# Order edges that hold background work behind a step's own operations, in a kernel of attention and two MoE layers on one core

## Chip, core and metric

One core of a Trainium2 chip runs the whole program in one launch. The metric is the device time in microseconds (us) of an execution; a kernel's time is the median of its runs.

## What is computed

Attention on q, k, v of 2 batches, 8 heads, 576 positions and 64 channels feeds a dense layer with a SiLU gate, and that one feeds four experts:

```python
q_d, k_d, v_d = (a.reshape(B, H, S // 4, 4, D).mean(axis=3) for a in (q, k, v))
out_up = np.repeat(sm_attn(q_d, k_d, v_d), 4, axis=2)
# local part: softmax over the keys with |i - j| < 4
x = (out_up + out_local).transpose(0, 2, 1, 3).reshape(1152, 512)
h = x @ w_in                                     # 512 x 2048
x = (h * (1.0 / (1.0 + np.exp(-h)))) @ w_out     # 2048 x 512
p = domain_probs / (domain_probs.sum(-1, keepdims=True) + 1e-09)
for e in range(4):                               # w1[e] 512 x 1024, w2[e] 1024 x 512
    out += p[:, e:e + 1] * (np.maximum(x @ w1[e], 0.0) @ w2[e])
```

## The kernel before

Every large product runs on TensorE (PE) from fp32 operands that are split in two: a rounded high part and the rest (h and l). A product is three matmuls, high by high, high by low and low by high (`mm3`, L468; `prod`, L667). A split is a copy on ScalarE (ACT) and a subtraction on VectorE (DVE) or POOL. The PSUM tiles of the first-layer products rotate over three banks (`mm_tile`).

The first layer runs in two halves of its 2048 hidden channels (`hf`), each over four chunks of tokens of 256, 320, 256 and 320 (`ci`). For a chunk, eight steps `g1_step` (12 matmuls) make a hidden tile each: ScalarE takes a Tanh (L487), VectorE makes the gate (L488), and one step later (`pend`, `flush`) ScalarE and VectorE split it (L493, L494). Four steps `g2_step` (24 matmuls) then multiply by w_out. In the first half ScalarE stores their result (L520), in the second VectorE adds it (L523), and ScalarE and VectorE split the sum as the experts' input (L524, L525).

An expert `e` takes four chunks of tokens (`ci`, 256 tokens, the last 384), and for each chunk four blocks of hidden channels (`k`). `first_products` makes a block (24 matmuls), ScalarE takes the ReLU (L644), four sums of quarter tiles follow (`SUMS`, L649: all on POOL for k of 0 and 1; for k of 2 and 3 three on VectorE and one on POOL), and ScalarE and VectorE split the result in two parts (L651, L652). `second_products` (21 matmuls, L667) multiplies seven combinations with seven w2 blocks, a block scheme that saves an eighth of the matmuls. `outputs` adds the chunk on VectorE (L693 to L728).

Beside the running step the weights are made ready. Pieces of the first layer's weights are loaded as 64-bit words and decoded (`split_raw`, L165 to L172). Pieces of the first expert's w1 come through the same queue of pieces (units 8 and 9, four pieces): a copy (L175) and a subtraction (L176), called by `split_ok` in the main loop once `limit` allows their unit. w2 blocks are loaded by `stage_ahead` (L558), which also makes the four block sums of a w2 block (L568, on POOL, for block 3 on VectorE) as soon as a block is staged and one of two `ks` tiles is free. `split_kk` splits a w2 block in four parts (L596; L598 on VectorE, the first part of each on POOL). `split_u` does the same for w1 of later experts (L580, L582).

No order is written out by hand: a scheduler places the instructions of each engine by data dependencies, by its own model of times and by a priority, which `prio` and `at_prio` set from a step's number. Each engine then runs its list strictly in that order.

## Time and profile before

| | us |
|---|---|
| median of 3 runs | 707.71 |
| lowest, highest of the runs | 705.44, 708.93 |
| profiled execution, its own time | 708.98 |
| its span from the first to the last instruction | 707.2 |

In the profile L12 is line 12 of the kernel. PE is the matmul, PEld the weight load of TensorE, SP the engine that issues the DMAs. A matmul's end in the profile is modelled, so that two in a row overlap. In the words after an instruction, [1.52 <-DVE gf L488] says that its engine had stood idle for 1.52 us and that an instruction of line 488 on VectorE ended that. Granted clock is the share of TensorE's full clock, 1.00 for the upper of its two levels and 0.50 for the lower.

### The profile page before, as it was taken

To read this page: it belongs to the slowest core of one execution; us is meant where nothing else is said; L and a number is where in the kernel's file an instruction comes from. 1 tells how busy PE (TensorE), PEld (TensorE's weight loads), DVE (VectorE), ACT (ScalarE), POOL (GpSimd) and SP (SyncE) were. 2 spreads that over 40 slices of the span, in tenths; PEclk is the share of its full clock that TensorE was granted. 3 is DMA by queue.
4 is the path that set the end of the run, shared out by engine and by line. 5 is a ranking of instruction groups with operands and counts; after the bars stand their busy time and mean duration, and the time that the engine had idled before them with its cause. 6 is when DMAs were issued, how large, how long until landed. Compare 5 with 4: busy or idle time off the path is not lost.

```text
span 707.2 us, 13791 instructions
## 1 busy us (share of the span) xinstructions
PE 668.5 (95%) x5516; PEld 649.8 (92%) x5516; DVE 445.1 (63%) x882; ACT 332.6 (47%) x753; POOL 248.9 (35%) x346
## 2 busy tenths in 40 slices
PE   5777999999989999998999999999999999999996
PEld 4565899999889999998999999999999999999995
DVE  5988747546864434674555886538866559755444
ACT  4667646457763422543334643335533356433321
POOL 4574442114420000365324482136542244322210
PEclk9978999999999999999999999999999999999999
DMA  9875532005461000032001420003210010000001
GB/s 260 246 220 196 164 94 64 22 12 168 137 201 32 1 1 1 1 123 87 1 1 33 139 69 1 1 1 112 99 31 1 1 53 9 1 32 16 17 31 44
DMA packets 16927, 48.16 MB, mean 68 GB/s; under 512 B 2976, under 2 KB 4256, under 8 KB 16864
## 3 DMA queue, kind: packets, MB, share of 16 engines
q1 hardware_dynamic: 16864, 47.29, 21.4%
q8 instruction: 43, 0.70, 0.4%
q14 instruction: 20, 0.16, 0.1%
HBM read 44.93 MB, written 2.36 MB: 67 GB/s over the span
## 4 chain that ended last, share of the span: by engine, by line
PE 79%; DMA 8%; DVE 6%; ACT 3%; issue 2%; POOL 2%; SPq 0%; DVEq 0%; POOLq 0%; ACTq 0%
PE mm L468 49%; PE p L667 25%; DMA stg<-in_w_dram 5%; DVE dec L169 2%; DMA kst<-in_w2d_dram 2%; DVE dec L167 1%; PE s L303 1%; POOL wbuf L172 1%; DMA vg<-in_va_dram 1%; PE o L395 1%; PE t L363 1%; ACT dec L165 1%; PE o L391 1%; DVE gl L494 1%; ACT stg L166 1%
## 5 line engine op out<-in xcount | busy, mean ns | idle before, releaser
L468 PE MATMUL mm<-xh,wbuf 128*128 128x256 f32 (+2 forms) x1280 | 274.6, 299 | 5.5 <-ACT xh L407 2.8
L468 PEld LDWEIGHTS mm<-xh,wbuf 128*128 128x128 f32 x1280 | 214.2, 192 | 7.2 <-DVE gf L488 3.6
L468 PE MATMUL mm<-xl,wbuf 128*128 128x256 f32 (+2 forms) x640 | 191.0, 299 | 0.0
L649 POOL TENSOR_TENSOR r<-r 128x128 f32<-128x128 f32 x160 | 93.5, 595 | 190.9 <-ACT r L644 150.9
L652 DVE TENSOR_TENSOR h<-r,h 128x384 fp32r<-128x384 f32 (+1 forms) x128 | 89.8, 702 | 72.5 <-ACT h L651 72.2
L468 PEld LDWEIGHTS mm<-xl,wbuf 128*128 128x128 f32 x640 | 122.5, 191 | 0.3
L651 ACT ACTIVATE h<-r 128x384 fp32r<-128x384 f32 (+1 forms) x128 | 73.9, 578 | 87.2 <-POOL r L649 57.2
L468 PE MATMUL mm<-gh,wbuf 128*128 128x256 f32 (+1 forms) x512 | 104.7, 297 | 0.9 <-ACT acc L520 0.9
L667 PE MATMUL p<-wext,h 128*128 128x256 f32 x672 | 96.1, 284 | 2.4 <-ACT h L651 2.4
L667 PEld LDWEIGHTS p<-wext,h 128*128 128x128 f32 x672 | 87.6, 191 | 2.8 <-ACT h L651 2.8
L667 PE MATMUL p<-wbuf,h 128*128 128x256 f32 x672 | 85.4, 280 | 0.0
L468 PEld LDWEIGHTS mm<-gh,wbuf 128*128 128x128 f32 x512 | 82.6, 188 | 1.2 <-ACT acc L520 1.2
L667 PEld LDWEIGHTS p<-wbuf,h 128*128 128x128 f32 x672 | 82.0, 188 | 0.0
L468 PE MATMUL mm<-gl,wbuf 128*128 128x256 f32 (+1 forms) x256 | 74.6, 297 | 0.0
L644 ACT ACTIVATE r<-mm 128x512 f32<-128x512 f32 x48 | 28.6, 597 | 82.4 <-PE mm L468 82.4
L649 DVE TENSOR_TENSOR r<-r 128x128 f32<-128x128 f32 x96 | 33.4, 348 | 40.7 <-ACT r L644 36.3
L494 DVE TENSOR_TENSOR gl<-gf,gh 128x256 fp32r<-128x256 f32 (+1 forms) x64 | 35.9, 562 | 19.6 <-ACT gh L493 19.4
L468 PEld LDWEIGHTS mm<-gl,wbuf 128*128 128x128 f32 x256 | 47.8, 188 | 0.1
L172 POOL TENSOR_TENSOR wbuf<-dec,wbuf 128x512 fp32r<-128x512 f32 x24 | 32.4, 1354 | 33.1 <-ACT wbuf L171 26.0
L598 POOL TENSOR_TENSOR wext<-kst,wext 128x512 fp32r<-128x512 f32 x8 | 10.6, 1325 | 85.0 <-issue 72.9
L695 DVE SCALAR_TENSOR_TENSOR acc<-p,pr,acc 128x256 f32<-128x256 f32 (+1 forms) x63 | 36.3, 604 | 6.5 <-PE p L667 6.5
L493 ACT ACTIVATE gh<-gf 128x256 fp32r<-128x256 f32 (+1 forms) x64 | 28.2, 441 | 19.0 <-DVE gf L488 19.0
(122 smaller groups left out, 989.0 us busy)
## 6 DMA issues: line engine op xcount, KB each, us to landing
stg<-in_w_dram SPq DMA_DIRECT2D x32, 512.0 KB
kst<-in_w2d_dram SPq DMA_DIRECT2D x16, 512.0 KB
kst<-in_w1d_dram SPq DMA_DIRECT2D x12, 512.0 KB
kq<-in_kqa_dram SPq DMA_DIRECT2D x8, 419.0 KB
kq<-in_kqb_dram SPq DMA_DIRECT2D x8, 323.0 KB
vg<-in_va_dram SPq DMA_DIRECT2D x8, 288.0 KB
stg<-in_w1d_dram SPq DMA_DIRECT2D x4, 512.0 KB
vw<-in_vb_dram SPq DMA_DIRECT2D x8, 180.0 KB
```

The source lines that it names most:

```text
L169: DVE.scalar_tensor_tensor(out=ai, in0=v[:, :, 1], scalar=-2 ** 31, in1=ai, op0=ALU.bitwise_and, op1=ALU.bitwise_or)
L172: POOL.tensor_tensor(out=l[:, c], in0=a, in1=h[:, c].bitcast(F32), op=ALU.subtract)
L468: ins = [PE.matmul(out=ps, lhsT=l, rhs=r, start=(first and i == 0), stop=(last and i == n - 1)) for i, (l, r) in enumerate(pairs)]
L493: ACT.activation(out=gh[ft][:, 0:n], in_=gf[:, 0:n], func=ACTF.Copy)
L494: DVE.tensor_tensor(out=gl[ft][:, 0:n], in0=gf[:, 0:n], in1=gh[ft][:, 0:n].bitcast(F32), op=ALU.subtract)
L598: eng.tensor_tensor(out=l[:, r], in0=x, in1=h[:, r].bitcast(F32), op=ALU.subtract)
L644: ACT.activation(out=r[:, 0:4].rearrange("p s t -> p (s t)"), in_=ps[:, 0:512], func=ACTF.Relu)
L649: (DVE if k in FAST_K and o != 7 else POOL).tensor_tensor(out=r[:, o], in0=r[:, a], in1=r[:, b], op=op)
L651: ACT.activation(out=h, in_=r[:, part], func=ACTF.Copy)
L652: DVE.tensor_tensor(out=l, in0=r[:, part], in1=h.bitcast(F32), op=ALU.subtract)
L667: ins = [PE.matmul(out=ps, lhsT=x, rhs=y, start=(opens and k == 0 and i == 0), stop=(k == 3 and i == n - 1), skip_group_check=True) for i, ...
L695: DVE.scalar_tensor_tensor(out=o, in0=ps, scalar=p, in1=o, op0=ALU.mult, op1=ALU.add)
```

## The change

A table `latest` keeps, for each engine, the last operation of the running step: the split of a hidden tile, of the first layer's sum, and the quarter sums and subtractions of an expert's block. `behind` adds an order edge from that operation to one of background work; the edge sets the order on the engine's list and adds no semaphore. Three kinds of background work get it: the pieces of the first expert's w1, the splits of w2 blocks 2 and 3 of the first expert, and all block sums. The pieces of w1 are besides taken up at four set steps, the odd ones of the second chunk in the second half, where `split_ok` had taken them up as they came. The block sums leave `stage_ahead` for a function `sum_ahead`, called at set places: for the first expert at the end of the first layer, for a later one in chunk 2 of the expert before (blocks 0 and 1) and in its chunk 3 after a w2 block was split (blocks 2 and 3).

```diff
--- before.py
+++ after.py
@@ -106,6 +106,18 @@
         return 96 + EXPERT * ((u - 8) // 2) + (0, 4)[u % 2]
 
 
+    latest = {}
+
+    def follow(i, earlier, reason):
+        tc.add_manual_dep(i.ins, earlier.ins.name, mybir.DependencyInfo(mybir.DependencyClass.NoSync, mybir.DependencyReason.DATA),
+                          reason=reason)
+
+    def behind(eng, i):
+        if eng in latest:
+            follow(i, latest[eng], "background work")
+        return i
+
+
 
     pieces = deque([(u, j) for u in range(8) for j in range(4)] + [(u, j) for u in range(8, 10) for j in range(2)])
     loaded = deque()
@@ -172,8 +184,8 @@
             POOL.tensor_tensor(out=l[:, c], in0=a, in1=h[:, c].bitcast(F32), op=ALU.subtract)
         else:
             c = slice(j * 1024, (j + 1) * 1024)
-            ACT.activation(out=h[:, c], in_=t, func=ACTF.Copy)
-            DVE.tensor_tensor(out=l[:, c], in0=t, in1=h[:, c].bitcast(F32), op=ALU.subtract)
+            behind(ACT, ACT.activation(out=h[:, c], in_=t, func=ACTF.Copy))
+            behind(DVE, DVE.tensor_tensor(out=l[:, c], in0=t, in1=h[:, c].bitcast(F32), op=ALU.subtract))
 
 
     actx = ExitStack()
@@ -289,8 +301,7 @@
 
 
     def after(i, earlier):
-        tc.add_manual_dep(i.ins, earlier.ins.name, mybir.DependencyInfo(mybir.DependencyClass.NoSync, mybir.DependencyReason.DATA),
-                          reason="PSUM bank")
+        follow(i, earlier, "PSUM bank")
 
     def local_scores(j):
         nb = j.nb
@@ -490,8 +501,8 @@
         flush()
 
         def fin():
-            ACT.activation(out=gh[ft][:, 0:n], in_=gf[:, 0:n], func=ACTF.Copy)
-            DVE.tensor_tensor(out=gl[ft][:, 0:n], in0=gf[:, 0:n], in1=gh[ft][:, 0:n].bitcast(F32), op=ALU.subtract)
+            latest[ACT] = ACT.activation(out=gh[ft][:, 0:n], in_=gf[:, 0:n], func=ACTF.Copy)
+            latest[DVE] = DVE.tensor_tensor(out=gl[ft][:, 0:n], in0=gf[:, 0:n], in1=gh[ft][:, 0:n].bitcast(F32), op=ALU.subtract)
 
         pend.append(fin)
 
@@ -521,8 +532,8 @@
         else:
             yf = tmp_p.tile([128, 320], F32, tag="gf", name="gf")
             DVE.scalar_tensor_tensor(out=yf[:, 0:n], in0=ps[:, 0:n], scalar=0.5, in1=ya, op0=ALU.mult, op1=ALU.add)
-            ACT.activation(out=xh[:, db, c], in_=yf[:, 0:n], func=ACTF.Copy)
-            DVE.tensor_tensor(out=xl[:, db, c], in0=yf[:, 0:n], in1=xh[:, db, c].bitcast(F32), op=ALU.subtract)
+            latest[ACT] = ACT.activation(out=xh[:, db, c], in_=yf[:, 0:n], func=ACTF.Copy)
+            latest[DVE] = DVE.tensor_tensor(out=xl[:, db, c], in0=yf[:, 0:n], in1=xh[:, db, c].bitcast(F32), op=ALU.subtract)
 
 
 
@@ -557,7 +568,10 @@
             with at_prio(need_of(e, x, k) - LEAD_KLOAD):
                 SP.dma_start(out=t.rearrange("p (s c) -> p s c", c=256) if x == "k" else t,
                              in_=w2d[e, k] if x == "k" else w1d[e, :, 1024 * k:1024 * k + 1024])
-        while sums_todo and sums_todo[0] in staged and ks_p and len(sums) < 2:
+
+    def sum_ahead(e, k):
+        if (e, k) in ((e, k) for e, x, k in sums_todo):
+            assert sums_todo[0] == (e, "k", k) and len(sums) < 2
             key = sums_todo.popleft()
             t = staged[key][0].rearrange("p (s c) -> p s c", c=256)
             c = sums[key] = ks_p[0].tile([128, 3, 256], F32, tag="ks", name="ks")
@@ -565,7 +579,7 @@
             with at_prio(need_of(*key) - LEAD_KSUM):
                 for o, a, b in ((c[:, 2], t[:, 3], t[:, 0]), (t[:, 3], t[:, 2], t[:, 3]),
                                 (c[:, 0], t[:, 2], c[:, 2]), (c[:, 1], t[:, 1], c[:, 0])):
-                    eng.tensor_tensor(out=o, in0=a, in1=b, op=ALU.subtract)
+                    behind(eng, eng.tensor_tensor(out=o, in0=a, in1=b, op=ALU.subtract))
 
     def home_u(k):
         h, l = slot(8 + k // 2)
@@ -593,9 +607,12 @@
         parts = (slice(2, 4), slice(4, 6), slice(0, 2), slice(6, 7))
         for part, (r, x) in enumerate(zip(parts, (t[:, 0:2], t[:, 2:4], c[:, 0:2], c[:, 2:3]))):
             with at_prio(tick_of(e, 0, k) + 6 - LEAD_KSPLIT):
-                ACT.activation(out=h[:, r], in_=x, func=ACTF.Copy)
+                a = ACT.activation(out=h[:, r], in_=x, func=ACTF.Copy)
                 eng = POOL if (k, part) in LO_ON_POOL else DVE
-                eng.tensor_tensor(out=l[:, r], in0=x, in1=h[:, r].bitcast(F32), op=ALU.subtract)
+                b = eng.tensor_tensor(out=l[:, r], in0=x, in1=h[:, r].bitcast(F32), op=ALU.subtract)
+                if e == 0 and k > 1:
+                    behind(ACT, a)
+                    behind(eng, b)
         wk[k] = (h, l)
         held[i] -= 1
         stage_ahead()
@@ -646,10 +663,11 @@
             with at_prio(p + d):
                 if n == 1:
                     for o, a, b, op in SUMS:
-                        (DVE if k in FAST_K and o != 7 else POOL).tensor_tensor(out=r[:, o], in0=r[:, a], in1=r[:, b], op=op)
+                        eng = DVE if k in FAST_K and o != 7 else POOL
+                        latest[eng] = eng.tensor_tensor(out=r[:, o], in0=r[:, a], in1=r[:, b], op=op)
                 h, l = (x[:, part.start - 1:part.stop - 1] for x in st.h)
                 ACT.activation(out=h, in_=r[:, part], func=ACTF.Copy)
-                DVE.tensor_tensor(out=l, in0=r[:, part], in1=h.bitcast(F32), op=ALU.subtract)
+                latest[DVE] = DVE.tensor_tensor(out=l, in0=r[:, part], in1=h.bitcast(F32), op=ALU.subtract)
 
     def bank(i):
         return pp_p[0].tile([128, 512], F32, tag=f"p{i}", name=f"p{i}")
@@ -789,7 +807,11 @@
                     g1_step(u0, ft, ci)
                 if hf == 0 and ci < 3:
                     attn_tick()
-                split_ok(limit[0])
+                if hf == 1 and ci == 1 and ft % 2:
+                    limit[0] = 10
+                    split_ok(10)
+                elif limit[0] < 10:
+                    split_ok(limit[0])
             flush()
             if hf == 0 and ci == 2:
                 close_attn()
@@ -798,19 +820,20 @@
                 u5_p[0].close()
                 ks_p.append(ctx.enter_context(tc.tile_pool(name="ks", bufs=2)))
                 stage_ahead()
-                for k in range(2):
-                    split_kk(0, k)
+                for k in range(4):
+                    sum_ahead(0, k)
+                    if k < 2:
+                        split_kk(0, k)
             if ci == 3:
-                limit[0] = 8 if hf == 0 else 10
+                limit[0] = 8
             for db in range(4):
                 next_step()
                 g2_step(u0 + 2, hf, db, ci)
                 if hf == 0 and ci < 2:
                     attn_tick()
-                split_ok(limit[0])
-                split_ok(limit[0])
-            if hf == 0 and ci == 3:
-                limit[0] = 10
+                if limit[0] < 10:
+                    split_ok(limit[0])
+                    split_ok(limit[0])
     while loaded:
         split_piece()
     m1ctx.close()
@@ -838,6 +861,8 @@
         second_products(st, ch)
         if ci == 3 and e < NE - 1:
             split_kk(e + 1, k)
+            if k < 2:
+                sum_ahead(e + 1, k + 2)
         if k == 3:
             outputs(e, ci, ch, p)
 
@@ -851,6 +876,8 @@
                 first_products(st)
                 if ci == 3 and e < NE - 1:
                     split_u(e + 1, k)
+                if ci == 2 and k % 2 == 0 and e < NE - 1:
+                    sum_ahead(e + 1, k // 2)
                 if before:
                     finish(*before, tick_of(e, ci, k) + (3 if ci == 3 else 2))
                 before = (st, ch)
```

Below, the lists of the engines as the build puts them, with line numbers of the file they are from (the changed file has L175 as L187, L487 as L498, L493 as L504, L520 as L531, L524 as L535, L568 as L582, L596 as L610, L644 as L661, L649 as L667, L651 as L669). Numbers behind a name tell apart tiles of one kind.

ScalarE before, from the last stores of the first half (acc) to the first steps of the second (th is a Tanh, gh a copy, stg a piece of w1, kst a block of w2):

```order
L520 ACTIVATE acc_75<-mm_2546 128x320
L175 ACTIVATE wbuf_76<-stg_2588 128x1024
L175 ACTIVATE wbuf_76<-stg_2623 128x1024
L175 ACTIVATE wbuf_76<-stg_2632 128x1024
L520 ACTIVATE acc_75<-mm_2590 128x320
L487 ACTIVATE th_2647<-mm_2634 128x256
L175 ACTIVATE wbuf_76<-stg_2653 128x1024
L493 ACTIVATE gh0_77<-gf_2648 128x256
L487 ACTIVATE th_2668<-mm_2655 128x256
L487 ACTIVATE th_2691<-mm_2678 128x256
L596 ACTIVATE wext_2122<-kst_2699 128x512
L493 ACTIVATE gh1_78<-gf_2669 128x256
```

The same place now:

```order
L531 ACTIVATE acc_75<-mm_2546 128x320
L531 ACTIVATE acc_75<-mm_2590 128x320
L498 ACTIVATE th_2647<-mm_2634 128x256
L504 ACTIVATE gh0_77<-gf_2648 128x256
L498 ACTIVATE th_2664<-mm_2651 128x256
L504 ACTIVATE gh1_78<-gf_2665 128x256
```

And where the pieces stand now, in the second chunk of the second half:

```order
L498 ACTIVATE th_2915<-mm_2902 128x320
L504 ACTIVATE gh0_77<-gf_2916 128x320
L187 ACTIVATE wbuf_76<-stg_2588 128x1024
L498 ACTIVATE th_2932<-mm_2919 128x320
L498 ACTIVATE th_2955<-mm_2942 128x320
L504 ACTIVATE gh1_78<-gf_2933 128x320
L504 ACTIVATE gh2_79<-gf_2956 128x320
L187 ACTIVATE wbuf_76<-stg_2623 128x1024
```

The four copies of w1 pieces left the first chunk for the second, and the w2 copy with them; their subtractions on VectorE moved alike.

ScalarE before, from the first layer's last splits (xh) to the first block of expert 0 (r is a block after the ReLU, h0 its high part, ks a block sum):

```order
L524 ACTIVATE xh_73<-gf_3733 128x320
L596 ACTIVATE wbuf_76<-kst_2722 128x512 x2
L596 ACTIVATE wbuf_76<-ks_3645 128x512
L596 ACTIVATE wbuf_76<-kst_3628 128x512 x2
L524 ACTIVATE xh_73<-gf_3762 128x320
L644 ACTIVATE r_3820<-mm_3823 128x512
L651 ACTIVATE h0_3821<-r_3820 128x384
L651 ACTIVATE h0_3821<-r_3820 128x512
L644 ACTIVATE r_3857<-mm_3860 128x512
```

The same place now:

```order
L535 ACTIVATE xh_73<-gf_3733 128x320
L535 ACTIVATE xh_73<-gf_3762 128x320
L610 ACTIVATE wbuf_76<-kst_3066 128x512
L610 ACTIVATE wbuf_76<-ks_3640 128x512
L610 ACTIVATE wbuf_76<-kst_3066 128x512
L610 ACTIVATE wbuf_76<-ks_3640 128x256
L610 ACTIVATE wbuf_76<-ks_3645 128x512
L610 ACTIVATE wbuf_76<-kst_3623 128x512 x2
L610 ACTIVATE wbuf_76<-ks_3645 128x256
L661 ACTIVATE r_3810<-mm_3813 128x512
L661 ACTIVATE r_3847<-mm_3850 128x512
L669 ACTIVATE h0_3811<-r_3810 128x384
```

All eight copies of w2 blocks 2 and 3 now follow the last split of the first layer and precede the first ReLU; before, three had run ahead of the third split. On TensorE's list 78 matmuls of first products stood ahead of the first second product, where there were 55.

POOL before, from the first quarter sums of expert 0 on (the ks and kst rows are block sums of expert 1):

```order
L649 TENSOR_TENSOR r_3820<-r_3820 128x128 x4
L649 TENSOR_TENSOR r_3857<-r_3857 128x128 x3
L568 TENSOR_TENSOR ks_3800<-kst_3786 128x256
L568 TENSOR_TENSOR ks_3815<-kst_3798 128x256
L649 TENSOR_TENSOR r_3857<-r_3857 128x128
L568 TENSOR_TENSOR kst_3786<-kst_3786 128x256
L568 TENSOR_TENSOR ks_3800<-kst_3786,ks_3800 128x256
```

POOL now, chunk 2 of expert 0, where these sums of block 0 come (r_4271 is its k of 0):

```order
L667 TENSOR_TENSOR r_4213<-r_4213 128x128
L667 TENSOR_TENSOR r_4271<-r_4271 128x128 x2
L582 TENSOR_TENSOR ks_4308<-kst_3786 128x256
L667 TENSOR_TENSOR r_4271<-r_4271 128x128
L582 TENSOR_TENSOR kst_3786<-kst_3786 128x256
L582 TENSOR_TENSOR ks_4308<-kst_3786,ks_4308 128x256
L667 TENSOR_TENSOR r_4271<-r_4271 128x128
L582 TENSOR_TENSOR ks_4308<-kst_3786,ks_4308 128x256
```

At the start of expert 0 no block sum is left on POOL's list; the eight quarter sums of its first two blocks stand there in one row.

## Rows read from the trace of the kernel before

**Rows 1.** the page's first part, busy us, share and instructions.

```profile
PE 668.5 (95%) x5516; PEld 649.8 (92%) x5516; DVE 445.1 (63%) x882; ACT 332.6 (47%) x753; POOL 248.9 (35%) x346
```

**Rows 2.** windows: length, busy us of PE PEld DVE ACT POOL, granted clock, DMA share, GB/s.

```profile
340.00:680.00 340.00, 340.00 (x2705) 340.00 (x2704) 217.68 (x415) 144.77 (x299) 133.62 (x190) 1.00 0.11 34
```

**Rows 3.** timeline of PE, ScalarE, VectorE, 204 to 230 us: start, duration, engine, line.

```profile
204.66 0.28 PE L468 MATMUL mm<-xh,wext 128*128 128x256 f32 x1
...
209.22 1.06 ACT L175 ACTIVATE wbuf<-stg 128x1024 fp32r<-128x1024 f32 x1 [1.36 <-DMA stg<-in_w1d_dram]
...
212.26 0.38 PE L468 MATMUL mm<-xh,u 128*128 128x256 f32 x1 [1.52 <-DVE gf L488]
...
212.86 0.63 ACT L596 ACTIVATE wext<-kst 128x512 fp32r<-128x512 f32 x1 [1.72 <-DMA kst<-in_w2d_dram]
...
230.38 0.42 DVE L523 SCALAR_TENSOR_TENSOR gf<-mm,acc 128x256 f32<-128x256 f32 x1 [1.55 <-PE mm L468]
```

**Rows 4.** two more windows, 206 to 216 and 314 to 330 us.

```profile
206.00:216.00 10.00, 8.01 (x64) 7.41 (x63) 6.63 (x10) 5.67 (x13) 1.29 (x1) 1.00 0.65 211
...
314.00:330.00 16.00, 13.65 (x98) 13.16 (x97) 7.87 (x12) 5.15 (x10) 10.88 (x17) 0.89 0.43 156
```

**Rows 5.** timeline, 308 to 333 us, the start of expert 0.

```profile
308.89 0.28 PE L468 MATMUL mm<-xh,wbuf 128*128 128x256 f32 x1
...
309.20 0.49 DVE L525 TENSOR_TENSOR xl<-gf,xh 128x320 fp32r<-128x320 f32 x1 [0.20 <-ACT xh L524]
...
313.95 0.48 DVE L523 SCALAR_TENSOR_TENSOR gf<-mm,acc 128x320 f32<-128x320 f32 x1
...
314.84 0.58 ACT L644 ACTIVATE r<-mm 128x512 f32<-128x512 f32 x1
...
322.83 1.41 POOL L568 TENSOR_TENSOR ks<-kst 128x256 f32<-128x256 f32 x2 [2.31 <-DMA kst<-in_w2d_dram]
...
324.68 0.63 ACT L651 ACTIVATE h<-r 128x512 fp32r<-128x512 f32 x1 [5.32 <-POOL r L649]
...
325.36 1.55 PE L667 MATMUL p<-wext,h 128*128 128x256 f32 x6 [1.95 <-ACT h L651]
...
332.42 0.28 PE L468 MATMUL mm<-xh,wbuf 128*128 128x256 f32 x1
```

**Rows 6.** chain of waits in order of time, two pieces of expert 0.

```profile
348.67 2.86 PE mm L468 x24
...
351.53 2.47 PE p L667 x21
```

**Rows 7.** timeline, one piece's subtraction, and steps of the second chunk.

```profile
207.31 1.23 DVE L176 TENSOR_TENSOR wbuf<-stg,wbuf 128x1024 fp32r<-128x1024 f32 x1 [0.52 <-ACT wbuf L175]
...
232.19 0.44 ACT L487 ACTIVATE th<-mm 128x320 f32<-128x320 f32 x1 [0.94 <-PE mm L468]
...
232.66 0.49 DVE L488 SCALAR_TENSOR_TENSOR gf<-th,mm 128x320 f32<-128x320 f32 x1 [0.95 <-ACT th L487]
...
233.95 0.44 ACT L487 ACTIVATE th<-mm 128x320 f32<-128x320 f32 x1 [0.30 <-PE mm L468]
```

**Rows 8.** groups of lines 598 and 568: duration ns minimum/median/maximum.

```profile
L598 DVE TENSOR_TENSOR wbuf<-kst,wbuf x8: 678/814/1755, 310.2 to 610.2; 128x512 fp32r<-128x512 f32 x8
...
L598 POOL TENSOR_TENSOR wbuf<-kst,wbuf x8: 1293/1491/1801, 309.8 to 606.1; 128x512 fp32r<-128x512 f32 x8
...
L568 POOL TENSOR_TENSOR ks<-kst,ks x24: 725/760/1185, 297.4 to 589.5; 128x256 f32<-128x256 f32 x24
```

**Rows 9.** timeline, chunk 2 of expert 0, its k of 0.

```profile
357.59 2.15 POOL L649 TENSOR_TENSOR r<-r 128x128 f32<-128x128 f32 x4 [4.77 <-ACT r L644]
...
360.85 0.67 DVE L652 TENSOR_TENSOR h<-r,h 128x512 fp32r<-128x512 f32 x1
...
362.47 0.42 DVE L728 TENSOR_TENSOR u<-u,p 128x256 f32<-128x256 f32 x1
...
364.43 0.88 PE L667 MATMUL p<-wext,h 128*128 128x256 f32 x6
```

## The prediction, made before the changed kernel had run

> **What bounds the kernel now.** I read the page's first part, then the stretches, then the order of the waits inside the two stretches that are not full. TensorE is the engine to watch: 668.5 of 707.2 us busy, with VectorE at 63% and POOL at 35% [rows 1]. From 340 to 680 us PE and its weight loads are full throughout [rows 2]. There nothing but fewer matmuls could help, and the change keeps all 5516. What it can move is the time in which PE stands still or runs at half clock inside the part that it reorders, and that is two stretches only. Everything up to about 203 us stands in the same order in both programs, and so does the tail.
>
> **First hole, 204 to 230 us (tokens 0 to 255 of the second half of the first layer).** PE starts the chunk at 204.66 and ends it just before the evacuation at 230.38 [rows 3]. The chunk has 8 tiles of 12 matmuls and 4 of 24, so 192, which is 8 times 24; 24 matmuls of that size take 2.86 us where nothing waits [rows 6], so the work is 22.9 us. It took 25.7, less some 0.1 for the last wait: 2.7 us lost. By the stretch from 206 to 216 weight loads idle 2.59 of 10 us [rows 4]. I take **2.6**. The rows say why: ScalarE sat 1.36 us on the DMA of a w1 piece, then copied it for 1.06 us (L175), with the running step's Tanh and copy behind it; PE then waited 1.52 us for a bank that L488 had to empty; next ScalarE sat 1.72 us on a w2 DMA (L596) in the same way [rows 3].
>
> **Second hole, 309 to 332 us (start of expert 0).** PE begins the first products at 308.89 and reaches those of chunk 1 at 332.42, 23.5 us [rows 5]. In between lie four first products (24 matmuls) and three second ones (21). In the steady part these take 2.86 and 2.47 us [rows 6], so the work is 4 x 2.86 + 3 x 2.47 = 18.9 us: **4.6 us lost**. The stretch agrees: from 314 to 330 weight loads idle 2.84 us, and at a mean granted clock of 0.89 another 0.11 x 16 = 1.8 us go [rows 4]; after the longer stop TensorE went to its lower level. The rows: POOL sat 2.31 us on the DMA of expert 1's w2, did two block sums (L568), and only then the last L649 of the running k, for which ScalarE waited 5.32 us and PE, behind ScalarE's L651, 1.95 us [rows 5]. Earlier, VectorE's w2 splits held L523 to 313.95 and so L644 to 314.84 [rows 5].
>
> **The change, part by part.**
>
> *The w1 pieces* (4 x L175, 4 x L176) and the w2 part behind them leave the first hole for the odd steps of the next chunk. So 2.6 us come back, if the new place can hold them. There a step takes 1.76 us of PE (233.95 less 232.19), VectorE's L488 0.49 of it and L494 as much, ScalarE's L487 0.44 and L493 about as much [rows 7]. Two steps with one piece: VectorE 1.96 + 1.23 = 3.19, ScalarE 1.8 + 1.06 = 2.9, of 3.52 us. With three banks PE needs a tile's bank two steps after the tile's end, 3.52 us; today the bank is free 0.96 us after the Tanh starts (232.66 + 0.49 less 232.19). Even with a copy and a subtraction wholly in front, 0.96 + 1.06 + 1.23 = 3.25 is still inside. Cost 0; the cover is the third bank, with 0.3 us to spare at worst.
>
> *The splits of w2 blocks 2 and 3* now stand behind the last L525. L523 then follows L525 at about 309.7 (309.20 + 0.49) in place of 313.95, L524 ends about 310.7, and ScalarE has all eight L596 in a row: six at 0.63 [rows 3] and two of half the size, some 0.4 us each, make 4.6 us, to 315.3. L644 of k = 0 (0.58) ends near 315.9, half a microsecond later than before [rows 5]. Before, PE would have run dry there; now its row holds three whole first products and six matmuls of the fourth ahead of any second product. Those keep it busy to 308.89 + 3 x 2.86 + 0.7 = 318.2, by which time two L644 and the first L651 (at most 0.63 [rows 5]) have ended, at about 317.1. VectorE has six L598, four at 0.68 [rows 8] and two of half the size at some 0.4, 3.5 us; they follow ScalarE's copies and end near 315.7. L652 (0.67 [rows 9]) runs from 317.1 to 317.8, and PE asks for it at 318.8, five second products later. Alongside POOL's two subtractions an L598 took up to 1.76 [rows 8]: two such cost 2.2 us, the first L652 ends near 318.6 and the next, if POOL's L649 slow these too, up to 1.3 later at 319.9, where PE asks at 319.4. Between 0 and 0.5 us, then; I take 0.5, since POOL is at work there without a pause.
>
> *The block sums of expert 1* leave the start of expert 0 altogether. POOL then does eight L649 without a pause, 8 x 0.54 (2.15 for four [rows 9]), from 315.9 to 320.2; the second half of k = 0 is split by about 321, and PE, with eleven second products and 17 matmuls of the fourth first product in hand, asks for it at 321.5 to 322. This closes the hole, 4.6 us.
>
> *Where the sums go.* In chunk 2 of experts 0, 1 and 2, three of the four sums of block 0 stand between L649s of k = 0. There L649 ends at 359.74 (357.59 + 2.15), L652 ends at 361.52, and PE wants that at about 364.43 [rows 9]. Three sums of 0.76 us [rows 8] make 359.74 into 362.0; L651 0.63 more; L652 is now put behind L728, which ends at 362.89, and ends at 363.6. Margin 0.8 us: cost 0. At block 1 the sums stand behind the only L649 of its step, with nothing waiting. Later experts lose as many sums from the start of each, where PE was full anyway: no gain.
>
> The SP queue gets two loads in the other order, both over 50 us ahead of use: 0. The edges carry no semaphore and add no instruction.
>
> **Sum.** The profiled execution took 708.98: 708.98 - 2.6 - 4.6 + 0.5 = 702.3. The median of the three runs, 707.71, is 1.3 lower. Both holes contain DMA waits (1.36, 1.72, 2.31 us), so part of those 1.3 may be smaller holes, which can't be won twice; I count half, 0.6, as lying elsewhere: **701.7 us**.
>
> **The rivals.**
>
> *Contention at the sums' new place.* VectorE's L598 with both operands on chip took 0.68 alone and up to 1.76 beside POOL [rows 8], and the sums now run beside the outputs of the chunk before. If each of the three sums held up a VectorE operation by its whole 0.76 us, L652 would end at 363.6 + 2.3 = 365.9, 1.5 past need, in three experts: +4.5, so 706; if each cost 0.5 us, 703.7. For: the margin is only 0.8. Against: the four L649 already ran beside those outputs, and L652 there took 0.67 [rows 9]. The Trainium skill (SBUF — State Buffer, "Who interferes with whom") states that a VectorE operation with two on-chip inputs and a GpSimd operation that reads there exclude each other for a whole instruction. The trace agrees in kind, not in size: at most 1.1 us of delay, where the POOL operation beside it takes 1.29 to 1.80, is not a whole one [rows 8].
>
> *Only one hole closes.* If the eight copies hold ScalarE past 317.5 (308.89 + 3 x 2.86), the fourth first product has no bank and PE stops as now. The plan has 315.9; 1.6 us of delay, such as a late w2 load, would do it. Then 708.98 - 2.6 - 1.3 = about 705.
>
> *The holes were this execution's.* It is the slowest of four; if the usual run loses 3 us in them instead of 7, the change gives about 705.
>
> *Slower: the w1 pieces jam the next chunk.* If VectorE's subtraction there takes over 0.3 us longer than 1.23 (a POOL subtraction of w2 lies near), L488 comes later than two steps, and PE stops in each of four places. A stop of 1.5 us as in the first hole [rows 3], with the clock falling as in the second (1.8 us), is 3.3; four are 13: 701.7 + 13 = about 715. Against it: POOL has one subtraction there in all.
>
> **How the numbers follow.** Both holes close, 699.5 to 703.5: 0.67. Contention, 703 to 706: 0.10, half of it under 704.2. One hole: 0.10. This execution's holes: 0.08. Jam: 0.05. A measurement of this kernel tells about 0.5%, 3.5 us: faster is below 704.2 and gets 0.67 + 0.05 less a little for the edge, 0.70; slower is above 711.2, 0.05; the rest, 0.25, is no change. The range runs from 699, the lower end of the first case, to 706, which takes in all cases but the jam.
>
> **What would show it.** Right: PE and weight loads read full in every 2 us stretch from 206 to 216 and from 314 to 330, the granted clock there is 1.00, no sum (L582 of the changed file) lies within 30 us of expert 0's start, the steps of chunk 1 keep 1.76 us. Wrong: PE waits on L661 or L670 near 318 us, or on L670 in chunk 2 of an expert; idle PE beside L188; or both holes closed and the time not below 704, which would put the loss ahead of 203 us.

## The result, and the profile after

The change makes the kernel faster: 701.4 us, median of 5 runs (699.02 to 702.26), against 707.71 (5 runs, 705.44 to 708.93); ratio 0.9909, 95% interval 0.988 to 0.9938. A second measurement (run 11) gave 700.31 against 707.89, ratio 0.9892 (0.9871 to 0.9912). A ratio is estimated over all runs of both kernels and need not be the quotient of the two medians. The profiled execution of the changed kernel took 701.93, its span is 699.9.

In the file after the change L468 is L479, L487 and L488 are L498 and L499, L493 is L504, L520 is L531, L523 to L525 are L534 to L536, L568 is L582, L596 and L598 are L610 and L612, L644 is L661, L649 is L667, L651 and L652 are L669 and L670, L667 is L685.

The page's first part, beside [rows 1]:

```profile
PE 668.9 (96%) x5516; PEld 650.9 (93%) x5516; DVE 442.8 (63%) x882; ACT 331.5 (47%) x753; POOL 246.1 (35%) x346
```

The windows of [rows 4] and [rows 2] (length, busy us of PE, PEld, DVE, ACT, POOL, granted clock, DMA share, GB/s):

```profile
206.00:216.00 10.00, 10.00 (x90) 10.00 (x90) 5.50 (x13) 5.30 (x14) 0.00 (x0) 1.00 0.01 5
...
314.00:330.00 16.00, 16.00 (x136) 16.00 (x135) 7.71 (x16) 5.85 (x11) 5.83 (x13) 1.00 0.20 74
340.00:680.00 340.00, 340.00 (x2693) 340.00 (x2692) 218.28 (x415) 143.78 (x301) 135.23 (x195) 1.00 0.11 34
```

Both holes are closed: weight loads are full, where 2.59 of 10 and 2.84 of 16 us stood idle, and the clock that was granted at 0.89 in the second is 1.00. All three windows are now alike.

The start of expert 0, timeline after the change (against [rows 5]):

```profile
307.09 0.48 DVE L534 SCALAR_TENSOR_TENSOR gf<-mm,acc 128x320 f32<-128x320 f32 x1
...
307.99 0.61 ACT L610 ACTIVATE wbuf<-kst 128x512 fp32r<-128x512 f32 x1
...
308.68 1.29 POOL L612 TENSOR_TENSOR wbuf<-kst,wbuf 128x512 fp32r<-128x512 f32 x1 [4.41 <-ACT wbuf L610]
...
309.15 1.37 DVE L612 TENSOR_TENSOR wbuf<-ks,wbuf 128x512 fp32r<-128x512 f32 x1 [0.55 <-ACT wbuf L610]
...
311.60 1.63 POOL L612 TENSOR_TENSOR wbuf<-kst,wbuf 128x512 fp32r<-128x512 f32 x1 [1.63 <-ACT wbuf L610]
...
311.73 1.18 ACT L661 ACTIVATE r<-mm 128x512 f32<-128x512 f32 x2
...
311.98 1.78 DVE L612 TENSOR_TENSOR wbuf<-kst,wbuf 128x512 fp32r<-128x512 f32 x1
...
312.81 0.93 ACT L669 ACTIVATE h<-r 128x384 fp32r<-128x384 f32 x2
...
313.18 4.66 POOL L667 TENSOR_TENSOR r<-r 128x128 f32<-128x128 f32 x8
```

POOL makes the eight quarter sums of two blocks without a pause, and the splits of w2 stand behind the last L534. PE has no stop here.

**Where the time went.** The first 175 us have the same order in nearly all these kernels, but took 171 to 178 us in different executions; that is what spreads the runs most. (Two profiled executions of the changed kernel have spans of 699.9 and 697.0 us, 2.8 apart, and the same 2.8 us lie ahead of their L531: 175.82 and 173.01.) So I measure three stretches inside each execution: A from the last store of the first half's third chunk to the last sum of the second half's first chunk (before: L520 at 175.14, L523 at 230.38 [rows 3]); B from there to the first sum of the last chunk (L523 at 300.90); C from there to the end of the span. Two of those rows in the timeline of before,

```profile
175.14 0.37 ACT L520 ACTIVATE acc<-mm 128x256 f32<-128x256 f32 x1
...
300.90 0.48 DVE L523 SCALAR_TENSOR_TENSOR gf<-mm,acc 128x320 f32<-128x320 f32 x1
```

and three in that of the changed kernel:

```profile
175.82 0.37 ACT L531 ACTIVATE acc<-mm 128x256 f32<-128x256 f32 x1
...
227.86 0.42 DVE L534 SCALAR_TENSOR_TENSOR gf<-mm,acc 128x256 f32<-128x256 f32 x1 [1.55 <-PE mm L479]
...
298.38 0.48 DVE L534 SCALAR_TENSOR_TENSOR gf<-mm,acc 128x320 f32<-128x320 f32 x1
```

| kernel, ratio to before (95%) | A | B | C |
|---|---|---|---|
| before | 55.2 | 70.5 | 406.3 |
| changed, 0.9909 (0.988 to 0.9938) | 52.0 | 70.5 | 401.5 |
| 1 no edges, 1.0001 (0.9982 to 1.0021) | 56.6 | 70.5 | 406.5 |
| 2 w1 part alone, 0.9965 (0.9947 to 0.9982) | 52.0 | 70.5 | 406.3 |
| 3 all but the w1 part, 0.993 (0.9908 to 0.9952) | 55.1 | 70.5 | 401.5 |
| 4 sums put back, 0.9889 (0.9865 to 0.9914) | 51.9 | 70.5 | 402.0 |
| 5 splits free, 0.9898 (0.9868 to 0.9927) | 51.7 | 70.5 | 402.6 |
| 6 w1 pieces two by two, 0.9884 (0.9859 to 0.9909) | 52.1 | 70.9 | 401.5 |
| 7 sums two by two, 0.9889 (0.9862 to 0.9915) | 51.9 | 70.5 | 401.6 |
| 8 decoding held back, 0.9859 (0.9833 to 0.9885) | 50.4 | 70.6 | 401.5 |
| 9 loads reordered, 0.9909 (0.9887 to 0.993) | 52.3 | 70.5 | 404.7 |
| 10 decoding spread, 0.9867 (0.9845 to 0.989) | 51.5 | 70.5 | 401.5 |
| 11 changed kernel again, 0.9892 (0.9871 to 0.9912) | 52.0 | 70.5 | 401.5 |
| 12 decoding earlier, 0.9861 (0.9836 to 0.9885) | 50.9 | 70.5 | 401.5 |

The change gains 3.2 us in A, 4.8 in C, 8.0 in all, and costs nothing in B. The profiled spans differ by 7.3, because the execution of before reached its L520 0.7 us earlier. Each row of the table is one execution.

Not all of the 4.8 us lies at the start of expert 0. The program's last four stores are issued at these places, in the timelines of before and of the changed kernel:

```profile
701.37 3.02 SPq L699 DMA_DIRECT2D out_dram<-acc  x4
```

```profile
694.34 3.02 SPq L717 DMA_DIRECT2D out_dram<-acc  x4
```

From the first sum of the last chunk (300.90, 298.38) up to these it is 400.5 and 396.0 us: 4.5 us of the gain. The other 0.3 us lies behind them, where the program ends; that stretch took 5.5 to 6.0 us in these kernels, and why it differs stays open.

### The profile page after: what moved, and what is told of

Its sections match the earlier page's. It is cut to its first block, busy times and chain, and to the rows that moved or that the text cites. A ratio compares the mean times of both kernels' runs of the same rounds, so it can differ in the third digit from the quotient of the medians.

```text
span 699.9 us, 13794 instructions
## 1 busy us (share of the span) xinstructions
PE 668.9 (96%) x5516; PEld 650.9 (93%) x5516; DVE 442.8 (63%) x882; ACT 331.5 (47%) x753; POOL 246.1 (35%) x346
## 4 chain that ended last, share of the span: by engine, by line
PE 82%; DMA 7%; DVE 4%; ACT 3%; issue 2%; POOL 2%; SPq 0%; DVEq 0%; POOLq 0%; ACTq 0%
PE mm L479 51%; PE p L685 26%; DMA stg<-in_w_dram 6%; DVE dec L181 1%; PE s L314 1%; POOL wbuf L184 1%; DMA vg<-in_va_dram 1%; PE o L406 1%; DVE dec L179 1%; PE t L374 1%; PE o L402 1%; ACT stg L178 1%; ACT dec L177 1%; DVE acc L713 1%; PE s L338 0%
## 5 line engine op out<-in xcount | busy, mean ns | idle before, releaser
L479 PE MATMUL mm<-xh,wbuf 128*128 128x256 f32 (+2 forms) x1280 | 274.3, 299 | 4.5 <-DVE gf L499 2.3
L479 PEld LDWEIGHTS mm<-xh,wbuf 128*128 128x128 f32 x1280 | 214.0, 192 | 6.5 <-ACT xh L418 3.1
L479 PE MATMUL mm<-xl,wbuf 128*128 128x256 f32 (+2 forms) x640 | 191.3, 299 | 0.0
L667 POOL TENSOR_TENSOR r<-r 128x128 f32<-128x128 f32 x160 | 93.0, 593 | 189.6 <-ACT r L661 149.9
L670 DVE TENSOR_TENSOR h<-r,h 128x384 fp32r<-128x384 f32 (+1 forms) x128 | 91.6, 718 | 65.8 <-ACT h L669 65.5
L479 PEld LDWEIGHTS mm<-xl,wbuf 128*128 128x128 f32 x640 | 122.8, 192 | 0.3
L669 ACT ACTIVATE h<-r 128x384 fp32r<-128x384 f32 (+1 forms) x128 | 73.2, 577 | 84.2 <-POOL r L667 53.9
L479 PE MATMUL mm<-gh,wbuf 128*128 128x256 f32 (+1 forms) x512 | 105.6, 298 | 0.9 <-ACT acc L531 0.9
L685 PE MATMUL p<-wext,h 128*128 128x256 f32 x672 | 93.3, 282 | 0.0
L685 PEld LDWEIGHTS p<-wext,h 128*128 128x128 f32 x672 | 86.0, 188 | 0.0
L685 PE MATMUL p<-wbuf,h 128*128 128x256 f32 x672 | 85.4, 280 | 0.0
L479 PEld LDWEIGHTS mm<-gh,wbuf 128*128 128x128 f32 x512 | 83.4, 190 | 1.2 <-ACT acc L531 1.1
L685 PEld LDWEIGHTS p<-wbuf,h 128*128 128x128 f32 x672 | 82.0, 188 | 0.0
L479 PE MATMUL mm<-gl,wbuf 128*128 128x256 f32 (+1 forms) x256 | 75.3, 299 | 0.0
L661 ACT ACTIVATE r<-mm 128x512 f32<-128x512 f32 x48 | 28.7, 598 | 82.3 <-PE mm L479 82.0
L667 DVE TENSOR_TENSOR r<-r 128x128 f32<-128x128 f32 x96 | 33.4, 348 | 41.1 <-ACT r L661 36.6
L479 PEld LDWEIGHTS mm<-gl,wbuf 128*128 128x128 f32 x256 | 48.4, 190 | 0.1
L612 POOL TENSOR_TENSOR wext<-kst,wext 128x512 fp32r<-128x512 f32 x8 | 10.6, 1324 | 81.9 <-ACT wext L610 43.8
L504 ACT ACTIVATE gh<-gf 128x256 fp32r<-128x256 f32 (+1 forms) x64 | 28.2, 442 | 16.2 <-DVE gf L499 15.7
```

What stands on the lines that cost most here:

```text
L479: ins = [PE.matmul(out=ps, lhsT=l, rhs=r, start=(first and i == 0), stop=(last and i == n - 1)) for i, (l, r) in enumerate(pairs)]
L504: latest[ACT] = ACT.activation(out=gh[ft][:, 0:n], in_=gf[:, 0:n], func=ACTF.Copy)
L612: b = eng.tensor_tensor(out=l[:, r], in0=x, in1=h[:, r].bitcast(F32), op=ALU.subtract)
L661: ACT.activation(out=r[:, 0:4].rearrange("p s t -> p (s t)"), in_=ps[:, 0:512], func=ACTF.Relu)
L667: latest[eng] = eng.tensor_tensor(out=r[:, o], in0=r[:, a], in1=r[:, b], op=op)
L669: ACT.activation(out=h, in_=r[:, part], func=ACTF.Copy)
```

## The experiments

Runs 1 to 4, 5 to 8, 9 to 11 and 12 were timed on four chips, each beside the kernel before.

**1. The edges, or the places of the calls?** `behind` returns its instruction without an edge:

```diff
-        if eng in latest:
-            follow(i, latest[eng], "background work")
```

> The changed kernel with every order edge left out and all calls at their new places. My theory: the calls alone move nothing, because the scheduler places background work by its priority; three w1 copies stand again ahead of the second half's first Tanh, and block sums of expert 1 ahead of the eighth quarter sum of expert 0. Both holes come back: weight loads idle 2 to 3 us in 206 to 216 us and again in 314 to 330, and the time is that of the kernel before, 706 to 709 us. Rival: the new places of the calls do the work and the edges only confirm them; then the time is that of the changed kernel, 700 to 703, and both stretches read full.

708.13 against 706.99 us, ratio 1.0001: nothing is left of the gain, and both holes are there (A 56.6, C 406.5). Windows of this run:

```profile
206.00:216.00 10.00, 8.18 (x56) 7.99 (x56) 6.73 (x13) 5.06 (x13) 1.29 (x1) 0.83 0.54 183
314.00:330.00 16.00, 12.90 (x101) 12.01 (x100) 7.29 (x11) 5.30 (x11) 11.00 (x17) 1.00 0.39 138
```

On all four compute engines and on SP the lists of this run are those of the kernel before, operation by operation, so that it is in effect a second execution of that kernel. Shown: without the edges the new places of the calls change nothing. Whether the edges do it with the calls at their old places is shown for the splits alone (run 4), whose calls never moved; for the w1 pieces and the sums it was not tried.

**2 and 3. Each part alone.** Run 2 is the kernel before with the w1 part; run 3 is the changed kernel without it:

```diff
-            behind(ACT, ACT.activation(out=h[:, c], in_=t, func=ACTF.Copy))
+            ACT.activation(out=h[:, c], in_=t, func=ACTF.Copy)
...
-                if hf == 1 and ci == 1 and ft % 2:
-                    limit[0] = 10
-                    split_ok(10)
-                elif limit[0] < 10:
-                    split_ok(limit[0])
+                split_ok(limit[0])
```

> The kernel before with the w1 pieces' part of the change alone. My theory: the first hole closes and is worth 2.6 us, so about 705 us (704.2 to 706), weight loads full in 206 to 216, the second stop at the start of expert 0 as it was. Rival (only the second hole matters, the first was one execution's): 707 to 708. Rival (pieces jam the second chunk of the second half): 708 or more, with PE idle beside L187 and L188.

> The changed kernel with the w1 pieces as before and all the rest kept. My theory: the second hole closes and is worth 4.6 us less 0 to 0.5, so about 703 us (702.5 to 704.5), weight loads full in 314 to 330 with the granted clock at 1.00, and 2 to 3 us idle in 206 to 216 as in the kernel before. Rival (the two parts are only worth something together): 706 or more. If both parts add, the gains of this run and of the w1 part alone sum to the 6.3 us of the whole change within 1.

704.16 and 702.01 against 706.99: 0.35% and 0.70%, about 2.5 and 4.9 us by the ratios. The sum, 7.4, lies between the two measurements of the whole change (6.4 and 7.6), and each part shortens its own stretch alone (A 52.0 with C 406.3; A 55.1 with C 401.5). Both medians came just under their ranges, in a series where the kernel before stood at 706.99. The parts add; the rivals fall.

**4. The sums put back.** They are made again in `stage_ahead`, as soon as a block is loaded, without edges:

```diff
-    def sum_ahead(e, k):
-        if (e, k) in ((e, k) for e, x, k in sums_todo):
...
+        while sums_todo and sums_todo[0] in staged and ks_p and len(sums) < 2:
...
-                    behind(eng, eng.tensor_tensor(out=o, in0=a, in1=b, op=ALU.subtract))
+                    eng.tensor_tensor(out=o, in0=a, in1=b, op=ALU.subtract)
```

> The changed kernel with the block sums made again as soon as a w2 block is loaded, and without edges; the w1 part and the edges on the w2 splits are kept. My theory: POOL's block sums at the start of expert 0 were the larger part of the second hole, so 2 to 4.6 us come back, 703.5 to 706 us: PE stops for L661's successors, with POOL waiting on a w2 DMA between two quarter sums, and the granted clock falls below 1.00 in 314 to 334. Rival: the w2 splits that held L523 and L644 were the cause, and the sums lay beside it; then the time stays at 701 to 702.5 and the stretch reads full.

699.45 us, ratio 0.9889, C 402.0. My theory fell: the sums are back among the quarter sums (here L664; L579 is the sum) and cost nothing there. Up to the last stores it is 396.0 us, as in the changed kernel; the 0.5 us more in C lie behind them. Timeline of this run:

```profile
304.00 0.48 DVE L534 SCALAR_TENSOR_TENSOR gf<-mm,acc 128x320 f32<-128x320 f32 x1
...
305.02 0.49 DVE L536 TENSOR_TENSOR xl<-gf,xh 128x320 fp32r<-128x320 f32 x1 [0.54 <-ACT xh L535]
...
305.58 0.33 SPq L569 DMA_DIRECT2D kst<-in_w1d_dram  x1
...
305.96 0.43 SPq L569 DMA_DIRECT2D kst<-in_w2d_dram  x1
...
310.08 1.51 POOL L664 TENSOR_TENSOR r<-r 128x128 f32<-128x128 f32 x2
...
311.56 1.05 POOL L579 TENSOR_TENSOR ks<-kst 128x256 f32<-128x256 f32 x1
...
312.57 1.61 POOL L664 TENSOR_TENSOR r<-r 128x128 f32<-128x128 f32 x3
```

The sum at 311.56 waits for no DMA. Its w2 block was asked for at 305.96, behind a w1 load that follows the first layer's last L536 (305.02). In run 2, where the splits stand as before (L609 is a split, L661 a quarter sum):

```profile
305.75 2.11 DVE L609 TENSOR_TENSOR wbuf<-ks,wbuf 128x256 fp32r<-128x256 f32 x2
...
307.78 0.48 DVE L534 SCALAR_TENSOR_TENSOR gf<-mm,acc 128x320 f32<-128x320 f32 x1
...
308.79 0.49 DVE L536 TENSOR_TENSOR xl<-gf,xh 128x320 fp32r<-128x320 f32 x1
...
308.92 0.81 SPq L569 DMA_DIRECT2D kst<-in_w1d_dram  x2
...
309.77 0.42 SPq L569 DMA_DIRECT2D kst<-in_w2d_dram  x1
...
316.74 1.42 POOL L579 TENSOR_TENSOR ks<-kst 128x256 f32<-128x256 f32 x2 [2.42 <-DMA kst<-in_w2d_dram]
...
318.12 0.45 POOL L661 TENSOR_TENSOR r<-r 128x128 f32<-128x128 f32 x1
...
319.29 0.98 PE L679 MATMUL p<-wext,h 128*128 128x256 f32 x6 [2.06 <-ACT h L663]
```

So the second hole was a chain of two links: VectorE's splits held the last L534, with it the loads of expert 1, and so the DMA for which a sum on POOL waited ahead of a quarter sum. The chain of waits of the kernel before has the same links (start, duration, engine, tile, line):

```profile
311.93 2.10 DVE wbuf L598 x2
...
315.96 6.74 DMA kst<-in_w2d_dram
...
322.83 1.41 POOL ks L568 x2
...
325.36 1.55 PE p L667 x6
```

Between the first two of these rows stand the last L523 (313.95 [rows 5]) and its L525.

**5. The splits free.** The edges on the splits of w2 blocks 2 and 3 are left out:

```diff
-                if e == 0 and k > 1:
-                    behind(ACT, a)
-                    behind(eng, b)
```

> The changed kernel without the edges on the splits of w2 blocks 2 and 3; the sums stay in their new places. My theory: the splits were the smaller part; L644 of the first block and the 55 matmuls of first products ahead of the first second product are as in the kernel before, POOL is free, and PE loses 0 to 1 us at the start of expert 0: 701 to 702.5 us. Rival: the splits were the larger part, 703.5 to 706 us, with a stop of PE of about 2 us near 318 us and a lower granted clock after it.

700.54 us, ratio 0.9898, C 402.6: 1.1 us more than the changed kernel, 0.8 of it ahead of the last stores, where 0 to 1 was expected. The long stop is gone and one of 0.42 is left, in the timeline of this run:

```profile
315.39 1.44 PE L682 MATMUL p<-wext,h 128*128 128x256 f32 x9 [0.42 <-ACT h L666]
```

Run 2 has neither measure, run 5 the sums away alone, run 4 the splits held back alone, and the changed kernel both. Of the 4.5 us ahead of the last stores the sums' move alone brings back 3.7 and the edges on the splits alone all 4.5; beside these edges the sums' move adds nothing that the stretch shows.

**9. The order of the loads alone.** Run 2, with the load of expert 1's second w2 block put behind its first one and a w1 load:

```diff
+            if (e, x, k) == (1, "k", 1):
+                follow(load[e, x, k], load[1, "u", 2], "load order")
```

> The kernel before with the w1 pieces' part, and one order edge on SP's queue: the loads of expert 1's w2 block 1 and of its last w1 block go behind that of its w2 block 0, as they do in the changed kernel and in the run with the sums put back. Sums and splits stay as in the kernel before. My new theory: POOL's wait of 2.3 us comes from SP, where the load of w2 block 0 (asked for by the sum) stands behind two loads that wait for buffers held by the splits; with that load some 6 us earlier the sum waits for nothing, the long stop of PE (about 2 us) goes and the time is 700 to 702 us, with a small stop left from L534 held by the splits (0.4 us as without the edges on the splits). Rival: the splits' edges closed the hole by putting first products ahead on PE; then the stop stays as in the run with the w1 part alone, 703 to 705 us.

701.11 us, ratio 0.9909, and 1.6 us by its stretch (C 404.7 against run 2's 406.3): about a third of the hole, so neither theory holds whole. The load moved much less than the 6 us that I had put down. Timeline of this run:

```profile
308.00 0.49 DVE L536 TENSOR_TENSOR xl<-gf,xh 128x320 fp32r<-128x320 f32 x1
...
308.57 0.33 SPq L570 DMA_DIRECT2D kst<-in_w1d_dram  x1
...
308.94 0.43 SPq L570 DMA_DIRECT2D kst<-in_w2d_dram  x1
...
314.81 0.80 POOL L582 TENSOR_TENSOR ks<-kst 128x256 f32<-128x256 f32 x1 [2.02 <-DMA kst<-in_w2d_dram]
...
318.62 0.98 PE L682 MATMUL p<-wext,h 128*128 128x256 f32 x6 [0.87 <-ACT h L666]
```

The load still follows the last L536 by a microsecond, and its sum comes 6.81 us after that L536, where run 2 had 7.95. So the load did not start sooner (0.94 us after L536, run 2's 0.98). With one w1 load just ahead of it in place of two, its sum began 5.87 us after it was issued, where run 2 had 6.97, and one sum (0.80) in place of two (1.42) then ran ahead of the quarter sum: the edge changed POOL's list too. These 1.1 and 0.6 us are about the 1.6. What remains is L534's delay, which only the edges on the splits remove. The runs' ratios set run 9 further below run 2 (0.9909, 0.9965) than the stretch does; they are from different chips, and I go by the stretch. Beside the changed kernel on its own chip run 9 is 1.2 us behind by the ratios and 3.4 by the stretches, and that difference stays open.

**6 and 7. Twice the load at a new place.** The four w1 pieces at two steps, and the sums of both blocks at one step of chunk 2:

```diff
-                if hf == 1 and ci == 1 and ft % 2:
+                if hf == 1 and ci == 1 and ft in (3, 7):
...
+                    split_ok(10)
```

```diff
-                if ci == 2 and k % 2 == 0 and e < NE - 1:
-                    sum_ahead(e + 1, k // 2)
+                if ci == 2 and k == 0 and e < NE - 1:
+                    sum_ahead(e + 1, 0)
+                    sum_ahead(e + 1, 1)
```

> The changed kernel with the four w1 pieces at two steps of the same chunk, two at a time, in place of four steps. My theory (a spare of 0.3 us at worst for one piece between two steps): two copies and a subtraction ahead of a step's gate, 0.96 + 2 x 1.06 + 1.23 = 4.3 us, are 0.8 over the two steps' 3.52, so PE stops up to 0.8 us in two places: 701.5 to 703.5 us. Rival (the order edges let the running step's Tanh and gate stand between the two pieces, so nothing is late): 700 to 702 with the chunk full. A third possibility, the clock falling after the stops, would give up to 1.8 us more for each: 705.

> The changed kernel with the sums of blocks 0 and 1 both at the first block of chunk 2. My theory (a margin of 0.8 us at that place): two more sums of 0.76 us stand between the quarter sums there, L652's successor comes 1.5 us later, 0.7 past need in three experts, so up to 2.1 us slower than the changed kernel, 701.4 to 703.5 us, with PE waiting on L669 or L670 in chunk 2. Rival (there is far more room than 0.8, since first products of the next block stand ahead of the second products on PE): no stop, 700.5 to 702. Contention between POOL and VectorE as I bounded it would give 703 to 706.

699.14 and 699.4 us. Two pieces in a row cost 0.4 us of stretch B, one wait of weight loads in the first of the two places and no fall of the clock, where one piece costs nothing. Timeline of run 6:

```profile
235.50 0.19 PEld L479 LDWEIGHTS mm<-xh,u 128*128 128x128 f32 x1 [0.34 <-DVE gf L499]
```

The end of the cover is there, between one piece and two. The doubled sums cost nothing that can be told (C 401.6 beside 401.5): the scheduler put six more matmuls of first products ahead on PE at the second block, so a margin worked out from the old order says little of a new one. The rival holds, and no cost of contention of the size that I had bounded shows.

**8, 10 and 12. A better version.** The changed kernel still has stops of 0.38, 0.98 and 0.87 us from 179 to 202 us, behind the decoding of the last two units of first-layer weights (6 and 7, eight pieces). Run 8 gives that the same edges:

```diff
+            hold_back = behind if u > 5 else (lambda eng, i: i)
...
-            ACT.activation(out=h[:, c], in_=a, func=ACTF.Copy)
+            hold_back(ACT, ACT.activation(out=h[:, c], in_=a, func=ACTF.Copy))
...
-            ACT.activation(out=ya, in_=ps[:, 0:n], func=ACTF.Copy, scale=0.5)
+            latest[ACT] = ACT.activation(out=ya, in_=ps[:, 0:n], func=ACTF.Copy, scale=0.5)
```

(the other decoding operations alike). Run 10 also calls the eight pieces at set steps, run 12 at earlier ones:

```diff
+                elif hf == 0 and ci == 3:
+                    if ft in (5, 7):
+                        split_ok(8)
...
-                    split_ok(limit[0])
+                    if ci != 3 or db == 2:
+                        split_ok(limit[0])
```

> The changed kernel with the same edges also on the decoding of the last two pieces of first-layer weights (units 6 and 7: L177 to L183) and on no other. In the changed kernel PE still stops three times between 179 and 202 us, 0.38, 0.98 and 0.87 us, behind such decoding. My theory: these stops close, 1.5 to 2.2 us come back, 699 to 700 us. Rival: the decoding moves so late that PE waits for the weights at the first w_out step of the second half near 220 us; then a stop of 1 to 3 us with a fall of the clock takes its place, 701 to 705 us.

> The run with the decoding of units 6 and 7 held back, with its eight pieces spread: two in steps of the first half's last chunk, five in its w_out steps (1, 1, 2, 1), one in the second half, in place of two in each w_out step. My theory: the stop of 0.7 us (weight loads 1.0) near 211 us in that run goes, since fewer pieces are left for the second half's first chunk: 0.5 to 1 us less than that run, 696.5 to 697.5 us, and weight loads full from 170 to 230. Rival: a piece in a step of the last chunk costs ScalarE 2.0 us beside the 1.8 of two steps, over their 3.52, and opens a stop there: 698 to 700.

> The changed kernel once more, beside the other two on the same chip: 699 to 702 us by its runs and those of the kernels that differ from it little; ratio to the kernel before 0.988 to 0.994.

> The spread decoding with its pieces called earlier: at the fifth and the seventh step of the first half's last chunk, then 2, 2, 1, 1 in its w_out steps, none in the second half. In the spread run PE still lost two stops of 0.77 and 0.64 us at 207 and 211 us, because a piece of a w_out step stands behind that step's own store and so two to three pieces run into the second half's first chunk. My theory: with two pieces called earlier the stops shrink to one of at most 0.7 us, 0.7 to 1.4 us less than the spread run, ratio to the kernel before 0.984 to 0.986 (696.5 to 698 us). Rival: VectorE is full there in any case (8.83 of 10 us busy) because its decoding operations take up to 1.80 us beside POOL's, and the stops stay: 698 to 699, ratio 0.9865.

Run 8: 697.78 us, ratio 0.9859, A 50.4: 1.6 us off the changed kernel's 52.0, as my theory had it. Its windows show PE full from 170 to 204 us, and a stop of 0.70 us where the pieces went:

```profile
170.00:204.00 34.00, 34.00 (x244) 34.00 (x244) 17.14 (x30) 20.42 (x43) 7.65 (x7) 1.00 0.30 93
206.00:216.00 10.00, 9.30 (x79) 8.96 (x78) 9.83 (x19) 8.03 (x20) 3.91 (x3) 1.00 0.45 125
```

Spreading gave nothing more: run 10 has A 51.5 and run 12 has 50.9, and their ratios, 0.9867 and 0.9861, can't be told from run 8's. In run 10 stops of 0.77 and 0.64 us stay, in run 12 of 0.88 and 0.22, so both theories fail. Run 12's rival holds. Run 10's rival has the time but not the place: the stops lie at 206 to 211 us, and PE is full from 170 to 204. Beside the changed kernel on the same chip run 10 has a median 1.9 us lower (698.37, 700.31), but the runs overlap (696.73 to 701.14, 698.65 to 701.54) and stretch A gives 0.5 us. All three stand below both kernels by their ratios, and run 8 is the best here, by stretch and by ratio; only run 10 was timed beside the changed kernel, which came out in run 11 as expected.

## Why the prediction was right, point by point

701.7 us was forecast, 699 to 706; 701.4 and 700.31 were measured. Both holes closed behind the edges, and no rival happened. The sizes were off, and the second hole's closing was put down to the wrong part of the change: that its return came out near the forecast is in part luck, since the change held two measures of which either nearly closes it.

- *First hole, 2.6 us.* Measured 3.2 in stretch A, 3.1 of it in the chunk itself. The next chunk's first matmul stands at this place in the timeline of before, and the chunk's and the next one's in that of the changed kernel:

```profile
230.17 0.31 PE L468 MATMUL mm<-xh,wext 128*128 128x320 f32 x1
```

```profile
205.26 0.28 PE L479 MATMUL mm<-xh,wext 128*128 128x256 f32 x1
...
227.66 0.31 PE L479 MATMUL mm<-xh,wext 128*128 128x320 f32 x1
```

That is 25.51 us before (from 204.66 [rows 3]) and 22.40 now. The mis-sized term is the chunk's work, 22.9 us: the 2.86 us for 24 matmuls are the experts', and here 24 take 2.80.

- *Second hole, 4.6 us less 0.5.* Measured 4.5 at this place (4.8 in stretch C, with the 0.3 behind the last stores), and PE has no stop there. The 0.5 was mis-sized: eight copies end at 311.8, 13.4 us after the chunk's first sum, where my plan had 315.3, 14.4 after it. They follow each other by 0.52 us, and I had counted 0.63 each. L661 came 0.6 us earlier than before against that sum (13.35, 13.94), not half a microsecond later.
- *The w1 pieces cost nothing.* Right: stretch B is 70.5 in both. Run 6 shows that the spare ended soon.
- *"The SP queue gets two loads in the other order: 0".* This step failed as an attribution: what the loads waited for, and their place, were part of the hole's cause (1.6 us with the order alone, run 9). In the changed kernel it did not show, since no sum waits there.
- *"This closes the hole, 4.6 us"*, said of the block sums' move, failed as an attribution too. *The edges on the splits*, which I had entered as a cost of up to 0.5, close the hole by themselves (run 4); the move alone leaves 0.8 (run 5). I had seen that L523 came late and had followed it only to L644, not to the buffers that wait for the last L525, the loads behind them and POOL.
- *The 0.6 us for the median.* I had let half of 1.3 us be smaller holes in the usual execution. Run 1 has both holes in full size (A 56.6, C 406.5) and run 2 the second (406.3); what differs most between executions is the first 175 us. With all terms as measured the sum would be 708.98 - 8.0 - 1.3 = 699.7, against 701.4 and 700.31: two holes too small and half of 1.3 too little together kept the forecast 2 us above that. That it is nearer the measured medians than the corrected sum is luck.
- *Contention.* No cost at the sums' new place (run 7). But I read the rule wrongly: see below.
- *The signs.* Windows and clock read as I had said. "No sum within 30 us of expert 0's start" was put too widely: expert 0's own sums still end about 2 us ahead of it, and those of expert 1, which I meant, begin at 351.39, 45 us behind it.

## What to carry to other kernels

Where PE is full nearly everywhere, look for its few stops and ask of each what stands ahead of the late operation in its engine's list; an order edge without a semaphore, from the step's last operation to background work, cost nothing and gave about 1% here, while moving the calls without it moved nothing. Follow a late operation past its next consumer: what frees a buffer also starts a load, and the stop may show on another engine. Two links of one chain don't add (3.7 and 4.5 of 4.5 us here), so take each away alone before naming the cause.

## What had not been expected of the hardware

**VectorE beside POOL.** I had said that a delay of 1.1 us beside a POOL operation of 1.29 to 1.80 is not a whole exclusion. The timeline after the change says otherwise: POOL's L612 runs from 308.68 to 309.97, VectorE's L612 from 309.15 to 310.52; the next pair from 311.60 to 313.23 and from 311.98 to 313.76. VectorE ends 0.55 and 0.53 us after POOL, where it takes 0.68 alone [rows 8]: nearly all of it lies behind POOL's end, and the delay is what was left of POOL's operation. The same in the timeline of run 8, on decoding:

```profile
208.58 1.39 POOL L185 TENSOR_TENSOR wbuf<-dec,wbuf 128x512 fp32r<-128x512 f32 x1 [3.14 <-ACT wbuf L184]
...
208.72 1.80 DVE L182 SCALAR_TENSOR_TENSOR dec<-stg,dec 128x512 int32<-128x512 int32 x1
```

POOL ends at 209.97, VectorE at 210.52. The Trainium skill (SBUF — State Buffer, "Who interferes with whom") calls the port pair that VectorE and GpSimd share an exclusive lock, for which a VectorE instruction with two SBUF inputs contends with a GpSimd instruction that reads there. These three pairs agree with it.

**The clock after a stop.** Before the change a stop of 1.95 us [rows 5] went with a granted clock of 0.89 in its window, which I counted as 1.8 us on top. In run 2 a stop of 2.06 us left it at 1.00, and stretch C is the same, 406.3 both times. What PE did otherwise there was to stop three more times, for 0.17 to 0.24 us (timeline of run 2):

```profile
320.55 0.98 PE L679 MATMUL p<-wext,h 128*128 128x256 f32 x6 [0.17 <-DVE h L664]
...
324.24 0.50 PE L679 MATMUL p<-wbuf,h 128*128 128x256 f32 x2 [0.24 <-ACT h L663]
...
324.96 1.46 PE L679 MATMUL p<-wbuf,h 128*128 128x256 f32 x10 [0.22 <-DVE h L664]
```

In the second hole, then, the time was the same with the fall as without it. Run 1, with the lists of the kernel before, has the fall in the other hole: behind a stop of 1.82 us in the first hole the granted clock of its window is 0.83, and stretch A is 56.6 us, where the kernel before and run 3 kept 1.00 in that window and took 55.2 and 55.1; in the second hole it stopped for 2.28 us, kept 1.00 and took 406.5 in C. So the fall went with 1.3 to 1.5 us more in the first hole and with nothing in the second. The cost of a fall was not tried by itself, and why the clock fell at one of these stops and not at another stays open.
